# Block-causal attention and a gated MLP on one core: score visits of two head pairs joined, and two more bank pairs for the value product

## The chip, the cores and the metric

The kernel runs on one core of one Trainium2 chip. The metric is the device time of one execution in microseconds; a run is told as the median of several executions. TensorE is called PE below, ScalarE ACT, VectorE DVE, GpSimd POOL, and SyncE, which issues most of the loads, SP.

## The reference

Block-causal attention (blocks of 64 positions) over 8 batches of 8 heads, 576 positions, head size 64, is followed by an MLP over all 4608 rows:

```python
scores = scale * np.matmul(q, k.transpose(0, 1, 3, 2))
mask = block_i >= block_j
scores = np.where(mask, scores, -1000000000.0)
attn = np.exp(scores - max) ; attn = attn / (sum(attn) + 1e-09)
attn_out = np.matmul(attn, v)
x = attn_out.transpose(0, 2, 1, 3).reshape(B * S, H * D)      # 4608 x 512
h = x @ w_in                                                   # 512 -> 2048
g = h * (1.0 / (1.0 + np.exp(-beta * h)))
out = g @ w_out                                                # 2048 -> 512
```

## The kernel before

**A planner writes the order.** The Python code first makes a list of operations (`P.op`), each with the engine that may run it, an estimated duration, what it depends on, the tiles that it uses and a priority. `Plan.schedule` then plays the clock forward: whenever an engine is free it takes, of the operations that are ready and whose buffers are free, the one with the lowest priority number. A tile gets its buffer when the first operation that uses it is placed, and gives it back after its last user. The result is one fixed order for each engine, with semaphore waits between engines. So a small edit to priorities, buffers or estimates can change the order of everything after it. An operation with another array shape (mode "row" for scoring, "full" for the rest) is held back by 0.25 of priority and planned with 140 ns on top (`SWITCH`).

**Attention.** The 8 heads of a batch are 4 pairs; u counts the 32 pairs, and pairs u and u+1 with even u are called a couple here. A couple shares the tile QKT, into which Q and K come transposed: in batches 0 and 1 by PE, from batch 2 (`QB`) on by a transposing DMA on SP (line 664), after casts on POOL (line 657). Per pair PE scores in four groups (lines 673 to 703, the matmuls in `fq` on line 696, and on line 440 where a loaded weight is used again): group 0 is the first block of 128 keys with its first 512 queries, group 1 its last 64 queries and the second key block, group 2 the third and fourth blocks, group 3 the last 64 keys. The two heads of a pair use the upper and the lower 64 rows of the array at the same time. Groups 0 to 2 use array tiles of 64 rows by 128 columns, group 3 tiles of 64 by 64. From batch 1 on the groups are placed as two operations, called visits here: (0, 1) and (2, 3). ACT then takes the exponential of each group (lines 710 and 722) into a tile E, of which there are three, DVE zeroes the masked corners (716, 718), PE multiplies by V (748, 30 matmuls), DVE takes the reciprocal of the row sums and normalises (760, 767), and the result xq is turned into xT: by PE (787) up to batch 2, by a transposing DMA on SP (774) from batch 3 on.

**MLP.** The 4608 rows are 9 chunks of 512. A chunk has 16 hidden groups of four matmuls (line 971), each followed by tanh on ACT (981) and a multiply on DVE (985). Chunk 0 then uses plain matmuls with w_out (1007); chunks 1 to 8 use a scheme with seven products of half-size blocks, each in two halves of eight matmuls (892), which needs sums of blocks on DVE (856) and additions when results are taken out of the banks (913 on ACT, 916 on DVE). Chunk r's hidden groups need xT of all batches that its rows come from; for chunks 3 to 7 that is batch r.

**PSUM.** There are eight banks. Scoring groups 0 to 2 and the value product take a tile "PP" of two neighbouring banks. A scoring PP may be on banks 0-1 or 2-3 (the lower pairs); the value product too from batch 1 on (except pair 3). Everything else (group 3, hidden groups, products) takes single banks "P1" of the upper four, 4 to 7; near the end, when no PP is left to place, of all eight. Of the products two sums stay in their banks over several products (tiles Z and Y, line 929).

**Priorities.** `pr(u)` (line 435) is 994 + 100 (b - 1.5) + 4.9 c for pair c of batch b from batch 2 on. The visit (0, 1) has pr(u) + .1, (2, 3) has pr(u) + .2, the value product pr(u) + .4. Hidden group j of chunk r has 1000 + 100 r + j, and most products of chunk r come at 1103 + 100 r and later. Batch b's attention thus stands ahead of the hidden groups of chunk b - 1 and behind those of chunk b - 2, and MLP work fills PE wherever attention waits.

The lines that place the visits and the value product:

```python
            te = P.tile("EX" if u == 3 else "E")
            ...
            for grp in GROUPS[b]:
                pst = [P.tile("PP" if g0 < 3 else "P1") for g0 in grp]
                ...
                o = P.op("PE", n, fq, deps=cps, tiles=pst + [tqk] + [te] * (b > 0),
                         lat=n + 200, mode="row", prio=pr(u) + .1 + .1*(grp[0] >= 2))
            ...
            pv.at = (4, 6, 0, 2) if u == 3 else (4, 6) if b < 1 else (0, 2)
```

Of the kernel before, what the change touches and what calls it, by code (L numbers as in the profile page):

```python
# [4 lines left out]
ACT = mybir.ActivationFunctionType  # L5
# [354 lines left out]
def bass_blockwise_causal_attn__then__act_swish_beta_kernel(  # L360
# [10 lines left out]
    with es:  # L371
# [4 lines left out]
        QB, XB, CAST = 2, 3, "POOL"  # L376
        NE = 3
        PARTS = [((0, 4, "SP", range(6)), (4, 8, "SP", range(2)), (4, 8, "POOL", range(2, 6)))] + [((0, 8, "SP", range(6)),)] * 7
        GROUPS = [((0,), (1,), (2,), (3,))] + [((0, 1), (2, 3))] * 7
        NS = 6  # L380
        NO = 4
        FAST = range(1, NRC)
        RX = 5 * RC
# [11 lines left out]
        QKT = [sb(f"QKT{i}", [128, 2, 2, 640], bf16) for i in range(3)]  # L395
# [5 lines left out]
        E4 = [e[:, 3072:3136] for e in Ef]  # L401
# [12 lines left out]
        PS = es.enter_context(nc.psum_tensor("PS", [128, 8, 512], f32))  # L414
# [4 lines left out]
        P = Plan()  # L419
# [15 lines left out]
        def pr(u):  # L435
            b, c = divmod(u, NPAIR)
            return u if b < 1 else 10 * u if b < 2 else 994 + 100 * (b - LAG) + 4.9 * c
        def again(g, o, i, x):

            return g.add_instruction(mybir.InstMatmult(  # L440
                start_tensor_calc=True, stop_tensor_calc=True, tile_size=i.tile_size, tile_position=i.tile_position,
                ldweights=False, name=nc.get_next_instruction_name(), engine=i.engine,
                ins=[g.lower_ap(x), i.ins[1]], outs=[g.lower_ap(o)]))

        def es_(te):
            return NE if te.cls == "EX" else te.slot


        def mk(fn):
            return lambda g, e: fn(g)  # L450
# [13 lines left out]
        for i in range(NQ):  # L464
# [5 lines left out]
            o = P.op("POOL", 200, mk(lambda g, i=i: g.memset(Vn[i][:, 4, :, 64:66], 0.0)), prio=-5)  # L470
# [6 lines left out]
        for i in range(NQ, NE + 1):  # L477
# [8 lines left out]
                  deps=[bt, c2], tiles=[tb], lat=400, mode="full", prio=5)  # L486
# [24 lines left out]
        for i in range(NFILL):  # L511
# [10 lines left out]
            n = 125  # L522
            o = P.op("PE", n, ff, deps=[c2, c4], tiles=[tf], lat=n, mode="full", prio=1e6 + i)
# [6 lines left out]
        for b in range(B):  # L530
            ts, t = P.tile("Vs"), P.tile("V")
# [3 lines left out]
            for h0, h1, e, tt in PARTS[b]:  # L535

                vs = []
                for i in tt:
# [9 lines left out]
                    n = (h1 - h0) / 8 * (1 if i < 4 else 0.25)  # L548
                    if e == "SP":
                        o = P.op("SP", 300 + 550 * n, fv, tiles=[ts], xfer=1400 * n,  # L550
                                 prio=3.5 + 0.1 * (h0 > 0) if b == 0 else 4 * b + (3.5 if b < 2 else 0.5),
                                 dma=["d_V", h0, 1])
                    else:
                        o = P.op("POOL", 150 + 1450 * n, fv, tiles=[t], xfer=1400 * n, prio=-30 if b == 0 else 4 * b + (3.5 if b < 2 else 0.5), dma=["d_VP", h0, 1])
# [8 lines left out]
                n = 5 if 4 in tt else len(tt)  # L563
                for g0 in range(h0, h1, 2):
                    g1 = g0 + 2

                    def fw(g, e, ts=ts, t=t, g0=g0, g1=g1, n=n):
                        return g.tensor_copy(Vn[t.slot][:, 0:n, g0:g1, 0:64], Vs[ts.slot][:, 0:n, g0:g1, :])  # L568

                    o = P.op("POOL", 60 + 60 * n * (g1 - g0), fw, deps=[*vs, *ones, *vzero], tiles=[ts, t],  # L570
                             prio=4 * b + 0.5 - (38.5 - 5 * (h0 > 0)) * (b < 1))
# [23 lines left out]
        for u in range(NU):  # L595
            b, c = divmod(u, NPAIR)
            Tv = tl[b]
            p = c % 2
# [5 lines left out]
            if b < QB:  # L604

                turned = []
                for w, (nm, src) in enumerate((("Q", q), ("K", k))):
# [7 lines left out]
                    o = ld[nm, u] = P.op("SP", 420, fl, tiles=[ts], xfer=1170, prio=u, dma=["d_S", 0, 1])  # L615
                    o.pkt = 80.0

                    def fn(g, e, ts=ts, tn=tn, p=p, w=w):
# [4 lines left out]
                    o = P.op("POOL" if onp else "DVE", 850 if onp else 750, fn, deps=[o], tiles=[ts, tn],  # L623
                             prio=-40 + 3 * u if onp else -1)

                    def ft(g, e, tn=tn, pt=pt, p=p, w=w):
                        for i in range(6):
# [4 lines left out]
                    o = P.op("PE", 6 * 43, ft, deps=[o, c4], tiles=[tn, pt, tt_], lat=6 * 43 + 170, mode="full",  # L632
                             prio=pr(u))
# [6 lines left out]
            elif p == 0:  # L640

                for w, (nm, src) in enumerate((("Q", q), ("K", k))):
                    ts = P.tile("S4")

                    def fl(g, e, ts=ts, src=src, b=b, c=c):
# [3 lines left out]
                    o = P.op("SP", QKI, fl, deps=[o for t in early6 for o in t.users] if b == QB else [],  # L649
                             tiles=[ts], xfer=QKX, prio=u, dma=["d_S4", 0, 1])  # L650
# [15 lines left out]

                turned = [P.op("SP", 3250, ft, deps=casts, tiles=[tt_, tn], xfer=3200, prio=-1, dma=["d_T", 0, 1])]
            tqk, cps = tt_, turned
            te = P.tile("EX" if u == 3 else "E")
            ex = []  # L670
            zs = []
            qk = {}
            for grp in GROUPS[b]:
                pst = [P.tile("PP" if g0 < 3 else "P1") for g0 in grp]

                def fq(g, e, pst=pst, grp=grp, tqk=tqk, p=p, b=b):
                    keep = {}
                    for g0, ps in zip(grp, pst):

                        held = g0 == 1 and 0 in grp  # L680
                        blocks = {0: [(0, 0, 512, 0)], 1: [(0, 512, 576, 448), (1, 128, 576, 0)],
                                  2: [(2, 256, 576, 0), (3, 384, 576, 320)], 3: [(4, 512, 576, 0)]}[g0]
                        for t, q0, q1, off in blocks:
                            m = min(128, 576 - 128 * t)
                            for h in range(2):
                                r = slice(64 * h, 64 * h + 64)
                                if g0 < 3:
                                    o = PS[0:m, ps.slot + h, off:off + q1 - q0]
                                else:
                                    o = PS[r, ps.slot, 0:64]  # L690
                                y = 64 * h * (b >= QB)
                                x = QKT[tqk.slot][r, p, 0, q0 + y:q1 + y]
                                if held and t == 0:
                                    z = again(g, o, keep[h], x)
                                    continue
                                z = g.matmul(o, QKT[tqk.slot][r, p, 1, 128 * t + y:128 * t + m + y], x)  # L696
                                if t == 0:
                                    keep[h] = z.ins
                    return z

                n = sum(220 if g0 < 3 else 60 for g0 in grp)
                o = P.op("PE", n, fq, deps=cps, tiles=pst + [tqk] + [te] * (b > 0),
                         lat=n + 200, mode="row", prio=pr(u) + .1 + .1*(grp[0] >= 2))
                for g0, ps in zip(grp, pst):
                    qk[g0] = o, ps
            for g0 in range(4):
                o, ps = qk[g0]
                if g0 < 3:
                    def fe(g, e, ps=ps, g0=g0, te=te):
                        return g.activation(E3[es_(te)][:, g0, :, :], PS[:, ps.slot:ps.slot + 2, :], ACT.Exp,  # L710
                                            scale=0.125)
                    x = P.op("ACT", act_t(1024), fe, deps=[o], tiles=[ps, te], lat=act_t(1024) + 93, prio=0)

                    def fz(g, e, g0=g0, te=te):
                        if g0 < 2:
                            return g.memset(E3[es_(te)][64:128, g0, :, 0:64], 0.0)  # L716
                        a = E3[es_(te)][64:128, 2, :, 0:64]
                        return g.memset(bass.AP(a.tensor, a.offset, [a.ap[0], [512, 2], [320, 2], [1, 64]]), 0.0)  # L718
                    zs.append(P.op("DVE", 160 if g0 < 2 else 220, fz, deps=[x], tiles=[te], prio=-20))
                else:  # L720
                    def fe(g, e, ps=ps, te=te):
                        return g.activation(E4[es_(te)][:], PS[:, ps.slot, 0:64], ACT.Exp, scale=0.125)
                    x = P.op("ACT", act_t(64), fe, deps=[o], tiles=[ps, te], lat=act_t(64) + 93, prio=0)
                ex.append(x)

# [11 lines left out]
            if u == 3:  # L737
                spare = te
            pv = P.tile("PP")
            pv.at = (4, 6, 0, 2) if u == 3 else (4, 6) if b < 1 else (0, 2)  # L740
            ti, tx = P.tile("inv"), P.tile("xq")

            def fav(g, e, te=te, pv=pv, Tv=Tv, c=c):
                for h in range(2):
                    for i in range(5):
# [7 lines left out]
                      lat=30 * 34 + 180, mode="full", prio=pr(u)+.4 + 5 * (b < 1))  # L753
# [8 lines left out]
            r = P.op("DVE", 150, fr, deps=[av], tiles=[pv, ti], prio=0)  # L762
# [6 lines left out]
            m = P.op("DVE", dve_t(640), fm, deps=[av, r], tiles=[pv, ti, tx], prio=0)  # L769
            m.same = [r]  # L770
            nrm = [m]
            if b >= XB:
                def fy(g, e, tx=tx, c=c, b=b):
# [4 lines left out]
                n = len(blocks(b))  # L778
                xt.append(P.op("SP", 1300 * n, fy, deps=nrm + (xt[u - 4:u - 3] if b > XB else []), tiles=[tx], xfer=1100,
                               prio=-1, dma=[f"d_TX{n}_", 0, n]))  # L780
# [179 lines left out]
        for r in range(NRC):  # L960
            row = RC * r
# [4 lines left out]
            for j in range(NJ):  # L966
                ph, tt = P.tile("P1"), P.tile("th")

                def fh(g, e, ph=ph, j=j, row=row):
                    for c in range(4):  # L970
# [4 lines left out]
                o = P.op("PE", 4 * mm(512), fh, deps=xd + [win[j // 4]], tiles=[ph, tg], lat=4 * mm(512) + 170,  # L975
                         mode="full", prio=1000 + 100 * r + j)
# [21 lines left out]
            for w, d0, d1 in [(w, 0, DM) for w in range(4)]:  # L998
# [4 lines left out]
                o = None  # L1003
                for j0, j1 in parts:
                    def fo(g, e, po=po, tg=tg, w=w, j0=j0, j1=j1, d0=d0, d1=d1):
                        for j in range(j0, j1):
# [4 lines left out]
                    n = (j1 - j0) * mm(d1 - d0)  # L1011
                    was = o
                    o = P.op("PE", n, fo, deps=gs[j0:j1] + wout[j0 // 4:(j1 + 3) // 4],
                             tiles=[po, tg], lat=n + 170, mode="full",
                             prio=1000 + 100 * r + (16 + w + 0.01 * j0 if w == 0 else
                                                     103 + 5.33 * (w - 1) + 1.33 * j0 / 4))
# [84 lines left out]
```

## Time and profile before

| what | us |
|---|---|
| median of 6 runs | 337.13 (336.88 to 341.67) |
| the profiled execution, its own time | 336.88 |
| its span in the trace | 335.0 |
| PE busy | 326.4 (97%) |
| DVE busy | 220.7 (66%) |
| ACT busy | 211.2 (63%) |
| POOL busy | 84.0 (25%) |
| exponentials of groups 0 to 2 (line 710), 93 of them | 91.8, 1.025 each |
| tanh (line 981), 144 | 96.5, 0.693 each |
| multiply after tanh (line 985), 144 | 95.5, 0.681 each |
| last scoring visit begins | 256.6 |

The profile is one execution, recorded by the hardware. The span is the time from its first to its last instruction; what lies between the span and the execution's own time is start and end of the program. A group of the profile is one line's instructions of one kind: how many, the union of their times, the mean of one in ns, and the idle time of the engine ahead of them with what ended it. Matmuls overlap in their pipeline, so their recorded durations add up to more than the time they take; the distance from one start to the next is the better measure, and the timeline merges neighbours of one line into one row with the first start, the length and the count. "PEld" is the loading of weights on PE, which runs beside its matmuls.

### The profile page before, as it was taken

The page shows a single profiled execution, that of the slowest core. Times are in us where ns is not written, and L with a number is a line of the kernel's source. Part 1 is how long each engine was busy: PE and PEld are TensorE (multiplying, and loading weights), DVE is VectorE, ACT ScalarE, POOL GpSimd, SP SyncE. Part 2 cuts the span into 40 slices and gives each one's busy share as a digit, 9 for nine tenths or more (in the row PEclk, how much of TensorE's full clock was granted, in tenths as well). Part 3 has the DMA queues.
Part 4 walks back from the last instruction along what each step waited for, and adds up shares of the span by engine and source line. Part 5 has one row for each costly group of instructions (what it writes and reads, how often), then busy time and mean ns, then how long its engine had stood idle before and what let it go on. Part 6 is the DMA issues. An engine that isn't in the chain of part 4 may idle for free.

```text
span 335.0 us, 7500 instructions
## 1 busy us (share of the span) xinstructions
PE 326.4 (97%) x3148; PEld 204.1 (61%) x3092; DVE 220.7 (66%) x449; ACT 211.2 (63%) x314; POOL 84.0 (25%) x127
## 2 busy tenths in 40 slices
PE   7999999999999999999999998999999999999996
PEld 4565465445576556756566674567556766666685
DVE  4647875668655788349875865577476866666742
ACT  2855974397665885686788557765877545544521
POOL 7656081055064027205320540510000000000000
PEclk9999999999999999999999999999999999999999
DMA  7999999899999999989699999975121201110023
GB/s 198 222 242 233 191 219 206 171 257 224 197 256 214 207 235 208 217 169 244 124 222 205 184 269 197 198 142 99 33 54 39 84 31 33 40 55 31 5 92 125
DMA packets 154993, 53.41 MB, mean 159 GB/s; under 512 B 139072, under 2 KB 154448, under 8 KB 154960
## 3 DMA queue, kind: packets, MB, share of 16 engines
q1 hardware_dynamic: 141200, 40.19, 63.9%
q10 hardware_dynamic: 8192, 8.39, 8.3%
q0 software_dynamic: 5568, 4.36, 8.3%
q8 instruction: 24, 0.39, 0.5%
q14 instruction: 9, 0.07, 0.1%
HBM read 36.71 MB, written 9.44 MB: 138 GB/s over the span
## 4 chain that ended last, share of the span: by engine, by line
PE 90%; DVE 3%; DMA 3%; ACT 2%; SPq 1%; issue 0%; POOL 0%
PE PS L971 37%; PE PS L892 29%; PE PS L748 9%; PE PS L696 8%; PE PS L1007 4%; DMA ST<-in_k_dram 2%; PE PS L519 2%; PE PS L787 1%; DVE gT L985 1%; ACT E L710 1%; PE PS L628 1%; DVE xq L767 1%; DMA xT<-xq 1%; SPq L612 1%; ACT th L981 1%
## 5 line engine op out<-in xcount | busy, mean ns | idle before, releaser
L971 PE MATMUL PS<-xT,w_in 128*128 128x512 bf16 x576 | 137.4, 380 | 1.3 <-DVE E L718 1.0
L981 ACT ACTIVATE th<-PS,beta 128x512 f32<-128x512 f32 x144 | 96.5, 693 | 64.6 <-PE PS L971 61.2
L985 DVE SCALAR_TENSOR_TENSOR gT<-th,PS 128x512 f16<-128x512 f32 x144 | 95.5, 681 | 40.0 <-ACT th L981 39.5
L710 ACT ACTIVATE E<-PS 128x1024 bf16<-128x1024 f32 x93 | 91.8, 1025 | 23.2 <-PE PS L696 22.4
L971 PEld LDWEIGHTS PS<-xT,w_in 128*128 128x128 bf16 x576 | 52.6, 98 | 57.7 <-issue 3.4
L892 PE MATMUL PS<-w_out,gT 128*128 128x256 f16 x512 | 63.2, 273 | 0.0
L892 PEld LDWEIGHTS PS<-w_out,gT 128*128 128x128 f16 x512 | 48.8, 98 | 11.8 <-DVE gT L985 0.6
L657 POOL CAST QKn<-ST 128x640 bf16<-128x640 f32 x48 | 36.8, 768 | 31.5 <-DMA ST<-in_k_dram 22.8
L568 POOL CAST Vn<-Vs 128x640 bf16<-128x640 f32 (+1 forms) x28 | 20.9, 746 | 91.5 <-DMA Vs<-in_v_dram 90.3
L696 PE MATMUL PS<-QKT 64*128 64x512 bf16 (+4 forms) x328 | 37.1, 297 | 0.4 <-DVE xq L767 0.3
L748 PEld LDWEIGHTS PS<-Vn,E 128*128 128x128 bf16 x930 | 31.5, 97 | 4.2 <-DVE xq L767 0.6
L913 ACT ACTIVATE ost<-PS 128x512 f32<-128x512 f32 x32 | 19.2, 599 | 22.8 <-PE PS L892 22.7
L748 PE MATMUL PS<-Vn,E 128*128 128x65 bf16 x930 | 32.8, 193 | 0.5 <-DVE xq L767 0.5
L892 PE MATMUL PS<-OV 128*128 128x256 f16 x256 | 32.1, 273 | 0.0
L696 PEld LDWEIGHTS PS<-QKT 64*128 64x128 bf16 (+1 forms) x328 | 13.4, 95 | 27.2 <-issue 15.8
L892 PEld LDWEIGHTS PS<-OV 128*128 128x128 f16 x256 | 24.3, 98 | 6.1 <-issue 0.4
L767 DVE TENSOR_TENSOR xq<-PS,inv 128x640 bf16<-128x640 f32 x32 | 26.2, 819 | 0.6
L716 DVE MEMSET E<- 64x64 uint32 x62 | 6.9, 112 | 26.2 <-ACT E L710 24.4
L856 DVE TENSOR_TENSOR OV<-gT 128x1024 f16<-128x1024 f16 x32 | 22.5, 710 | 1.1 <-PE PS L892 0.6
L916 DVE SCALAR_TENSOR_TENSOR ost<-PS,ost 128x512 f32<-128x512 f32 x22 | 15.1, 685 | 5.5 <-PE PS L892 4.8
L892 PE MATMUL PS<-OV,gT 128*128 128x256 f16 x128 | 16.0, 273 | 0.0
L1007 PE MATMUL PS<-w_out,gT 128*128 128x512 f16 x64 | 15.3, 380 | 0.0
(61 smaller groups left out, 174.7 us busy)
## 6 DMA issues: line engine op xcount, KB each, us to landing
out_dram<-ost ACTq DMA_DIRECT2D x32, 256.0 KB, 3.2
ST<-in_q_dram SPq DMA_DIRECT2D x12, 576.0 KB, 6.0
ST<-in_k_dram SPq DMA_DIRECT2D x12, 576.0 KB, 7.8
Vs<-in_v_dram SPq DMA_DIRECT2D x24, 256.0 KB, 4.6
ST<-in_q_dram SPq DMA_DIRECT2D x8, 288.0 KB, 6.2
ST<-in_k_dram SPq DMA_DIRECT2D x8, 288.0 KB, 6.8
w_in<-in_moe_w_in_dram POOLq DMA_DIRECT2D x4, 512.0 KB, 10.9
w_out<-in_moe_w_out_dram POOLq DMA_DIRECT2D x4, 512.0 KB, 10.0
```

What stands on the lines that cost most here:

```text
L568: return g.tensor_copy(Vn[t.slot][:, 0:n, g0:g1, 0:64], Vs[ts.slot][:, 0:n, g0:g1, :])
L657: return g.tensor_copy(QKn[tn.slot][:].rearrange("p a w n -> p (a w n)")[:, 640 * (2 * a + w):][:, 0:640] .rearrange("p (t h d) -> p t h d ...
L696: z = g.matmul(o, QKT[tqk.slot][r, p, 1, 128 * t + y:128 * t + m + y], x)
L710: return g.activation(E3[es_(te)][:, g0, :, :], PS[:, ps.slot:ps.slot + 2, :], ACT.Exp, scale=0.125)
L748: z = g.matmul(o, eblk(te, t, i, h), Vn[Tv.slot][:, t, 2 * c + h, 0:65], start=(t == 0), stop=(t == i))
L767: return g.tensor_tensor(xq[tx.slot][:].rearrange("p i (h d) -> p h i d", h=2), both(pv, 0, 64), x, ALU.mult)
L856: return P.op("DVE", dve_t(SZ * HC / 2), mk(lambda g: g.tensor_tensor(fo(), fx(), fy(), op)), deps=deps, tiles=tiles, prio=prio)
L892: x = g.matmul(PS[:, pw.slot, HM * w:HM * w + HM], fa()[:, j, 128 * w:128 * w + 128], fb()[:, j, :], start=first and (pair or w == 0) and ...
L971: z = g.matmul(PS[:, ph.slot, :], w_in[:, c, 128 * j:128 * j + 128], xT[:, c, row % RX:row % RX + RC], start=(c == 0), stop=(c == 3))
L981: return g.activation(th[tt.slot][:], PS[:, ph.slot, :], ACT.Tanh, scale=beta[:, j:j + 1])
L985: return g.scalar_tensor_tensor(out=gT[tg.slot][:, j, :], in0=th[tt.slot][:], scalar=1.0, in1=PS[:, ph.slot, :], op0=ALU.add, op1=ALU.mult)
L1007: z = g.matmul(PS[:, po.slot, 0:d1 - d0], gT[tg.slot][:, j, 128 * w:128 * w + 128], w_out[:, j, d0:d1], start=(j == 0), stop=(j == NJ - 1))
```

## The change

For batches 2 to 7 (`JOIN`) a couple's visits are placed together, when the loop is at its first pair. There are three: (0, 1) of pair u; groups 2 and 3 of u and then groups 2 and 3 of u+1 in one operation; (0, 1) of pair u+1. The middle one has priority pr(u) + .2, the others pr(u) + .1 and pr(u+1) + .1. It takes two PP tiles and a single bank that both pairs' group 3 share (64 columns each), and the E tiles of both pairs. The exponential of group 3 reads its pair's 64 columns. The value product of batches 2 to 7 may be placed on banks 4-5 or 6-7 if neither lower pair is free. All matmuls, exponentials and transfers are the same in number and shape. In batches 0 and 1 the visits are as before; only group 3 of an odd pair uses the other 64 columns of its bank.

```diff
+        JOIN = (2,3,4,5,6,7)
...
-            te = P.tile("EX" if u == 3 else "E")
...
-            for grp in GROUPS[b]:
-                pst = [P.tile("PP" if g0 < 3 else "P1") for g0 in grp]
...
-                n = sum(220 if g0 < 3 else 60 for g0 in grp)
-                o = P.op("PE", n, fq, deps=cps, tiles=pst + [tqk] + [te] * (b > 0),
-                         lat=n + 200, mode="row", prio=pr(u) + .1 + .1*(grp[0] >= 2))
+            if b not in JOIN or p == 0:
+                tes = {uu: P.tile("EX" if uu == 3 else "E") for uu in ((u,) if b not in JOIN else (u, u + 1))}
+                qks = {uu: {} for uu in tes}
+                visits = [[(u, g) for g in grp] for grp in GROUPS[b]] if b not in JOIN else [
+                    [(u, 0), (u, 1)], [(u, 2), (u, 3), (u + 1, 2), (u + 1, 3)], [(u + 1, 0), (u + 1, 1)]]
+                for grp in visits:
+                    small = P.tile("P1") if any(g0 == 3 for _, g0 in grp) else None
+                    pst = [P.tile("PP") if g0 < 3 else small for _, g0 in grp]
...
+                                    if g0 < 3:
+                                        o = PS[0:m, ps.slot + h, off:off + q1 - q0]
+                                    else:
+                                        o = PS[r, ps.slot, 64 * (uu % 2):64 * (uu % 2) + 64]
...
+                    n = sum(220 if g0 < 3 else 60 for _, g0 in grp)
+                    o = P.op("PE", n, fq, deps=cps, tiles=list({id(x): x for x in pst}.values()) + [tqk] + [tes[uu] for uu in sorted({uu for uu, _ in grp})] * (b > 0),
+                             lat=n + 200, mode="row", prio=pr(u) + .2 if len(grp) == 4 else pr(u + 1) + .1 if grp[0][0] > u else
+                             pr(u) + .1 + .1 * (grp[0][1] >= 2))
...
-                        return g.activation(E4[es_(te)][:], PS[:, ps.slot, 0:64], ACT.Exp, scale=0.125)
+                        return g.activation(E4[es_(te)][:], PS[:, ps.slot, 64 * p:64 * p + 64], ACT.Exp, scale=0.125)
...
-            pv.at = (4, 6, 0, 2) if u == 3 else (4, 6) if b < 1 else (0, 2)
+            pv.at = (4, 6, 0, 2) if u == 3 else (4, 6) if b < 1 else (0, 2, 4, 6) if b in JOIN else (0, 2)
```

More of the change, by code (lines that the diff above doesn't have):

```diff
@@ L668, in bass_blockwise_causal_attn__then__act_swish_beta_kernel @@
             tqk, cps = tt_, turned
-            te = P.tile("EX" if u == 3 else "E")
             ex = []
             zs = []
-            qk = {}
-            for grp in GROUPS[b]:
-                pst = [P.tile("PP" if g0 < 3 else "P1") for g0 in grp]
[L676 to L699, printed above, removed]
-                n = sum(220 if g0 < 3 else 60 for g0 in grp)
-                o = P.op("PE", n, fq, deps=cps, tiles=pst + [tqk] + [te] * (b > 0),
-                         lat=n + 200, mode="row", prio=pr(u) + .1 + .1*(grp[0] >= 2))
-                for g0, ps in zip(grp, pst):
-                    qk[g0] = o, ps
@@ new lines, in bass_blockwise_causal_attn__then__act_swish_beta_kernel, with fq @@
+            if b not in JOIN or p == 0:
[6 more added lines that the diff above has]
+                    pst = [P.tile("PP") if g0 < 3 else small for _, g0 in grp]
+                    def fq(g, e, pst=pst, grp=grp, tqk=tqk, b=b):
+                        keep = {}
+                        for (uu, g0), ps in zip(grp, pst):
+                            held = g0 == 1 and (uu, 0) in grp
+                            blocks = {0: [(0, 0, 512, 0)], 1: [(0, 512, 576, 448), (1, 128, 576, 0)],
+                                      2: [(2, 256, 576, 0), (3, 384, 576, 320)], 3: [(4, 512, 576, 0)]}[g0]
+                            for t, q0, q1, off in blocks:
+                                m = min(128, 576 - 128 * t)
+                                for h in range(2):
+                                    r = slice(64 * h, 64 * h + 64)
+                                    if g0 < 3:
+                                        o = PS[0:m, ps.slot + h, off:off + q1 - q0]
+                                    else:
+                                        o = PS[r, ps.slot, 64 * (uu % 2):64 * (uu % 2) + 64]
+                                    y = 64 * h * (b >= QB)
+                                    x = QKT[tqk.slot][r, uu % 2, 0, q0 + y:q1 + y]
+                                    if held and t == 0:
+                                        z = again(g, o, keep[h], x)
+                                        continue
+                                    z = g.matmul(o, QKT[tqk.slot][r, uu % 2, 1, 128 * t + y:128 * t + m + y], x)
+                                    if t == 0:
+                                        keep[h] = z.ins
+                        return z
+                    n = sum(220 if g0 < 3 else 60 for _, g0 in grp)
+                    o = P.op("PE", n, fq, deps=cps, tiles=list({id(x): x for x in pst}.values()) + [tqk] + [tes[uu] for uu in sorted({uu for uu, _ in grp})] * (b > 0),
+                             lat=n + 200, mode="row", prio=pr(u) + .2 if len(grp) == 4 else pr(u + 1) + .1 if grp[0][0] > u else
+                             pr(u) + .1 + .1 * (grp[0][1] >= 2))
+                    for (uu, g0), ps in zip(grp, pst):
+                        qks[uu][g0] = o, ps
@@ L706, in bass_blockwise_causal_attn__then__act_swish_beta_kernel @@
+            te, qk = tes[u], qks[u]
             for g0 in range(4):
@@ L720, in bass_blockwise_causal_attn__then__act_swish_beta_kernel, with fe @@
                 else:
-                    def fe(g, e, ps=ps, te=te):
-                        return g.activation(E4[es_(te)][:], PS[:, ps.slot, 0:64], ACT.Exp, scale=0.125)
+                    def fe(g, e, ps=ps, te=te, p=p):
+                        return g.activation(E4[es_(te)][:], PS[:, ps.slot, 64 * p:64 * p + 64], ACT.Exp, scale=0.125)
                     x = P.op("ACT", act_t(64), fe, deps=[o], tiles=[ps, te], lat=act_t(64) + 93, prio=0)
```

## The prediction

> **What bounds the kernel now.** I read the page first: busy shares, clock row, chain.
>
> ```profile
> span 335.0 us, 7500 instructions
> ...
> PE 326.4 (97%) x3148; PEld 204.1 (61%) x3092; DVE 220.7 (66%) x449; ACT 211.2 (63%) x314; POOL 84.0 (25%) x127
> ...
> PEclk9999999999999999999999999999999999999999
> ...
> PE 90%; DVE 3%; DMA 3%; ACT 2%; SPq 1%; issue 0%; POOL 0%
> ...
> L710 ACT ACTIVATE E<-PS 128x1024 bf16<-128x1024 f32 x93 | 91.8, 1025 | 23.2 <-PE PS L696 22.4
> ...
> L767 DVE TENSOR_TENSOR xq<-PS,inv 128x640 bf16<-128x640 f32 x32 | 26.2, 819 | 0.6
> ```
>
> PE is busy 97% at an undisturbed clock and holds 90% of the chain of waits. Batches 0 and 1 are untouched, so the stretch that matters begins with the first visit of batch 2, at 67 us. Stage table, from there to the end of attention and on to the end (columns: PE, PEld, DVE, ACT, POOL busy, clock, DMA):
>
> ```profile
> 67.00:262.00 195.00, 193.27 (x1939) 118.37 (x1889) 132.58 (x277) 139.92 (x208) 52.55 (x68) 1.00 0.95 180
> 262.00:335.00 73.00, 70.25 (x507) 49.18 (x505) 45.07 (x71) 32.16 (x49) 0.00 (x0) 1.00 0.18 57
> ```
>
> PE lacks 1.7 us of 195; ACT and DVE are at 72% and 68%. After 262 us PE runs projections alone. So the time is PE's work plus PE's waits, and only two things can move it: how long PE takes for a visit, and where it stands still. That attention finishes earlier or later is worth nothing in itself, because hidden groups and products fill PE meanwhile.
>
> "Busy" hides the losses inside a visit, so I went to the starts of single matmuls in the trace. Full-array matmuls start 0.109 us apart at 256 columns and 0.216 at 512. What exceeds that is a wait or a change of tile shape. From 67 us on ten waits of over 0.06 us add up to 2.9: 1.20 at 204.55, 0.37 at 102.50, 0.37 at 166.10, the other seven 1.0 together.
>
> **The switch, measured.** Two single visits of groups 2 and 3, with eight products' matmuls between them (timeline of PE):
>
> ```profile
> 127.81 1.80 PE L892 MATMUL PS<-w_out,gT 128*128 128x256 f16 x15
> 129.54 0.54 PE L696 MATMUL PS<-QKT 64*128 64x320 bf16 x6
> 130.02 1.05 PE L892 MATMUL PS<-w_out,gT 128*128 128x256 f16 x8
> 131.00 0.54 PE L696 MATMUL PS<-QKT 64*128 64x320 bf16 x6
> 131.47 0.72 PE L892 MATMUL PS<-w_out,gT 128*128 128x256 f16 x5
> ```
>
> From 130.02 to 131.00 is 0.98; eight matmuls are 0.87; so entering the visit costs 0.10. From 129.54 to 130.02 is 0.47 (unrounded). A single visit therefore costs 0.57. The plan of before already puts two such visits back to back three times (near 90, 175 and 201.5 us). One of them:
>
> ```profile
> 174.46 0.59 PE L971 MATMUL PS<-xT,w_in 128*128 128x512 bf16 x2
> 174.99 1.01 PE L696 MATMUL PS<-QKT 64*128 64x320 bf16 x12
> 175.93 0.50 PE L892 MATMUL PS<-w_out,gT 128*128 128x256 f16 x3
> ```
>
> From 174.99 to 175.93 is 0.94, plus 0.10 for the entry: 1.04. This is exactly the twelve-matmul middle visit of the change, so its price needs no guess: 2 x 0.57 - 1.04 = 0.10 saved.
>
> **The change, part by part.**
>
> *Visits joined.* No matmul is added or removed. Twelve couples of pairs (batches 2 to 7, two each) go from four visits to three. Counting a visit as one entry (0.10) and one exit (0.12 after a 64x64 tile), twelve would save 12 x 0.22 = 2.6 us. The Trainium skill speaks against that count: its page "TensorEngine Tiling (Array Packing)", section "Tiling Modes", says that changing the tile shape makes the array drain. In a visit the shape changes again, since groups 0 to 2 use 64x128 tiles and group 3 uses 64x64. The trace agrees: 64x128 to 64x64 costs 0.09, and in the row at 174.99 the step from pair u's 64x64 tiles to pair u+1's 64x128 costs 0.12, as much as a leave would. Listed as (2, 3, 2, 3), the joined visit has five shape changes where two single ones have six. I take the row: 0.097 each. Three of the twelve are joined already, so nine are gained: 9 x 0.097 = **0.87 us**, all on PE, which sets the end. By the entry-and-exit count on all twelve the time would be 334.5.
>
> *Order.* In before, groups 2 and 3 of both pairs often run between the two pairs' groups 0 and 1 already, so the change mostly fixes an order that is there. Moved earlier with the joined visit is pair u+1's E slot: two of three slots are taken at once. No DMA is reordered by the code: loads on SP keep their priority, V's casts stay on POOL, and the transposes of Q and K serve both pairs of a couple already. Hidden by PE's fill; if the cover goes, a late E slot delays the next couple's first visit by at most a value product with normalising, about 2 us of attention, not of PE.
>
> *A new wait.* Groups 2 and 3 needed one lower pair of banks; joined they need both, and one upper bank. So the visit may wait for one exp more, 1.02 (L710), and its own first exp starts 0.47 later (0.94 of PE, not 0.47). That is 0.5 to 1.5 us per couple, 1 to 3 us per batch. Behind it in the schedule stand exps, the value product (L748), normalising, the transposing DMA (L774), then the hidden groups (L971) of the chunk that needs the batch. PE itself is given other work by the planner, which knows these banks; counting L892's matmuls in the trace, 5 to 12 products of 0.87 of the earlier chunks are still undone when chunks 3 to 6 begin. On PE I take **0**; bounds below.
>
> *Value products on upper banks.* They can start without waiting for a scoring pair. The wait that this could remove is the one at 102.50, whose releaser is the normalising that empties a lower pair:
>
> ```profile
> 102.50 0.39 PE L696 MATMUL PS<-QKT 64*128 64x512 bf16 x2 [0.30 <-DVE xq L767]
> ...
> 166.10 0.82 PE L971 MATMUL PS<-xT,w_in 128*128 128x512 bf16 x3 [0.20 <-DMA xT<-xq]
> ...
> 199.90 2.17 SPq L774 DMA_TRANSPOSE xT<-xq  x1
> ...
> 204.55 0.81 PE L971 MATMUL PS<-xT,w_in 128*128 128x512 bf16 x3 [1.03 <-DVE E L718]
> ```
>
> It is worth 0.37, with 0.07 at 96.92. In exchange an upper pair is gone for 0.92 (L748) + 0.22 (L760) + 0.82 (L767) + about 0.1 between them = 2.1 us. The lower pairs come first in the list, so I expect few upper ones. I take 0; bounds -0.4 and +4.8 (the squeeze, below).
>
> The named releaser at 204.55 misleads: hidden groups don't read E. The last transpose of batch 5 was issued at 199.90 and landed 4.6 us later, at 204.5. So that wait, like 166.10, is for xT.
>
> **Sum.** Span 335.0 - 0.87 = 334.1; 1.9 lies around it (336.88 - 335.0): 336.0 for the profiled execution. The median of the runs is 0.25 above that execution, so **336.3 us**. The waits of 2.9 us bound the unknown downwards; with all of them gone it would be 333.4.
>
> **Rivals.**
>
> *Waits go too.* An upper bank is freed (one for both group 3s, not two), scoring doesn't wait for normalising, and xT comes in time at 166 and 204.5. For it: those waits total 2.0 us and depend on the order. Against: a new order makes waits of its own, and the planner's order of before already leaves only 1.1% of this stretch. Time: 337.1 - 0.87 - 2.0 = 334.2.
>
> *xT late.* The joined visit's longer chain makes chunks 3 to 6 start on an xT that the planner believed landed. For it: the plan counts 0.56 for this visit's matmuls, and 0.95 for an exp that takes 1.025; 204.55 shows that a misjudged landing costs 1.2. Against: the misjudged part is only about 0.5 per visit, and the planner puts undone products in front while it waits for xT. If all four boundaries cost 1.2: 4.8 in place of 1.6, so +3.2 - 0.87: 339.4, still within 1%.
>
> *Bank squeeze (the other side).* Place: the upper four banks. The products' sums (line 929) hold one or two for many visits, a value product takes two for 2.1 us, and then no hidden group can start. The same page of the skill, section "Restrictions and Gotchas", says that row tiling raises the pressure on PSUM since each row tile writes a bank of its own; five of eight banks now go to one visit. It gives no price; the rows do: of 2.1, PE spends 0.92 on the value product and 0.87 on a product, if one is ready, leaving 0.3 to 0.4 idle, and 1.2 if none is. With 12 of the 24 up there at 0.4 each, 4.8 - 0.87 = +3.9: 341.1. It makes the change a loss once these idles pass 0.87, and a loss of over 1% once they pass 4.2. Against: an upper pair is taken only when both its banks are free.
>
> *No change at all.* If the plan, unasked, had joined as many, nothing would be gained; it did so three times of twelve, so at least nine are new.
>
> **Chances.** Forecast 0.5 (335.2 to 337.6, waits between -1.1 and +1.3 of today's), waits go 0.15, xT late 0.2, squeeze 0.15. A measurement of this kernel can tell about 1% from no change, that is 3.4 us: below 333.8 lies only the end of the second case, 0.04; above 340.5 the squeeze and the tail of xT late, 0.14; within, 0.82. The range takes in most of the second and third cases: 334.0 to 340.4.
>
> **What would show it.** Right: no scoring visit of group 2 alone after 67 us, twelve visits of twelve matmuls of 1.04 each, nine visits fewer, PE's waits after 67 us still near 3 us. Wrong: waits before L971 released by L985 or L767 (banks: squeeze); waits before the first L971 of a chunk when an L774 lands (xT late); joined visits that cost other than 1.04; PE's streaming time changed. If the time moves by over 1 us, I expect waits to account for it, not switches.

## The result, and the profile after

The changed kernel takes 335.99 us in the median (35 runs) beside 337.54 us for the kernel before in the same comparison: a ratio of 0.9951, 95% interval 0.9935 to 0.9967. That is about 1.65 us, where 0.87 was forecast. (The ratio leaves out the few executions that took over 1.5% longer than their kernel's quickest; the medians, over all, differ by 1.55.) Line numbers have moved: loads of Q and K are L647 (was L646), scoring is L701 (was L696), and from there on lines stand seven later: exponentials L717, the value product L755, normalising L774, the transposing DMA of xT L781, products L899, hidden groups L978, their multiply L992 (L993 in the kernels with a hold).

The page of the changed kernel:

```profile
span 332.9 us, 7496 instructions
...
PE 324.3 (97%) x3148; PEld 204.4 (61%) x3092; DVE 220.0 (66%) x449; ACT 210.4 (63%) x314; POOL 84.6 (25%) x127
...
PE 83%; DMA 5%; ACT 4%; DVE 3%; SPq 2%; issue 1%; POOL 0%; ACTq 0%
```

PE's busy time fell by 2.1 us, just as the span did, and it is still busy 97%: the bound is the same. The share of DMA in the chain that ended last rose from 3% to 5%.

One joined visit on PE's timeline:

```profile
183.79 1.04 PE L899 MATMUL PS<-w_out,gT 128*128 128x256 f16 x8
184.76 1.01 PE L701 MATMUL PS<-QKT 64*128 64x320 bf16 x12
185.70 1.04 PE L978 MATMUL PS<-xT,w_in 128*128 128x512 bf16 x4
```

Eight matmuls at 0.109 begin at 183.79, so the visit costs 0.10 to enter and 0.94 until the next full matmul starts. Twelve visits of twelve matmuls stand in the trace (three before) and no visit of groups 2 and 3 of one pair is left after 67 us.

I split the stretch from the first visit of batch 2 to the start of PE's last matmul into waits (distance between two starts, less streaming, less the shape change; those over 0.06 us) and the rest. Distances that fit one matmul missing from the trace are left out of the waits.

| us | to last matmul | waits | rest |
|---|---|---|---|
| before | 264.4 | 2.9 | 261.5 |
| changed | 262.5 | 2.2 | 260.3 |

The stretch is 1.9 shorter: 1.15 in the rest, 0.75 in waits. The other 0.3 of the span's 2.1 lies ahead of batch 2, where the two kernels do the same work, and says nothing of the change. In the rest, nine visits saved are 9 x 0.097 = 0.87; a further 0.2 comes from one joined visit that follows directly on a PE transpose of 64 rows (103.69 us), so that neither a leave nor an entry is paid there. The waits changed places more than they shrank. For 166.10 (0.37) and 204.55 (1.20) there are now 0.24 at 168.81 and 0.53 at 205.49, both for xT, and a new one of 0.59 at 77.07, where a hidden group waits for the multiply L992, which gives a bank back (the last xT that chunks 4 and 5 need landed at 168.76 and 205.44, just ahead of the two):

```profile
77.07 0.61 PE L978 MATMUL PS<-xT,w_in 128*128 128x512 bf16 x2 [0.43 <-DVE gT L992]
...
168.81 0.61 PE L978 MATMUL PS<-xT,w_in 128*128 128x512 bf16 x2
...
205.49 0.82 PE L978 MATMUL PS<-xT,w_in 128*128 128x512 bf16 x3 [0.37 <-DMA xT<-xq]
```

The bracket shows only the idle part after the modelled end of the matmul before; the distances between starts give the larger numbers above.

### The profile page after: what moved, and what is told of

The parts are those of the page before. It is cut to its first block, busy times and chain, and to the rows that moved or that the text cites. A ratio compares the mean times of both kernels' runs of the same rounds, so it can differ in the third digit from the quotient of the medians.

```text
span 332.9 us, 7496 instructions
## 1 busy us (share of the span) xinstructions
PE 324.3 (97%) x3148; PEld 204.4 (61%) x3092; DVE 220.0 (66%) x449; ACT 210.4 (63%) x314; POOL 84.6 (25%) x127
## 4 chain that ended last, share of the span: by engine, by line
PE 83%; DMA 5%; ACT 4%; DVE 3%; SPq 2%; issue 1%; POOL 0%; ACTq 0%
PE PS L978 35%; PE PS L899 26%; PE PS L755 8%; PE PS L701 7%; PE PS L1014 4%; ACT E L717 3%; DMA Vs<-in_v_dram 2%; DMA xT<-xq 2%; SPq L543 1%; PE PS L794 1%; ACT th L988 1%; DMA ST<-in_k_dram 1%; DVE gT L992 1%; PE PS L629 1%; DVE OV L863 1%
## 5 line engine op out<-in xcount | busy, mean ns | idle before, releaser
L978 PE MATMUL PS<-xT,w_in 128*128 128x512 bf16 x576 | 137.3, 380 | 1.0 <-DVE gT L992 0.4
L992 DVE SCALAR_TENSOR_TENSOR gT<-th,PS 128x512 f16<-128x512 f32 x144 | 95.9, 681 | 36.8 <-ACT th L988 35.9
L717 ACT ACTIVATE E<-PS 128x1024 bf16<-128x1024 f32 x93 | 91.8, 1026 | 28.6 <-PE PS L701 28.0
L978 PEld LDWEIGHTS PS<-xT,w_in 128*128 128x128 bf16 x576 | 52.7, 98 | 56.9 <-DVE gT L992 2.4
L899 PE MATMUL PS<-w_out,gT 128*128 128x256 f16 x512 | 63.3, 273 | 0.0
L899 PEld LDWEIGHTS PS<-w_out,gT 128*128 128x128 f16 x512 | 49.1, 98 | 12.5 <-issue 0.8
L658 POOL CAST QKn<-ST 128x640 bf16<-128x640 f32 x48 | 38.0, 792 | 23.6 <-DMA ST<-in_k_dram 12.9
L701 PE MATMUL PS<-QKT 64*128 64x320 bf16 (+4 forms) x328 | 36.5, 297 | 0.4 <-ACT E L717 0.4
L755 PEld LDWEIGHTS PS<-Vn,E 128*128 128x128 bf16 x930 | 31.1, 97 | 3.7 <-DVE xq L774 0.6
L755 PE MATMUL PS<-Vn,E 128*128 128x65 bf16 x930 | 32.2, 193 | 0.7 <-DVE xq L774 0.5
L899 PE MATMUL PS<-OV 128*128 128x256 f16 x256 | 32.1, 273 | 0.0
L701 PEld LDWEIGHTS PS<-QKT 64*128 64x128 bf16 (+1 forms) x328 | 13.4, 95 | 25.6 <-issue 10.3
L899 PEld LDWEIGHTS PS<-OV 128*128 128x128 f16 x256 | 24.6, 98 | 6.3 <-issue 0.6
L774 DVE TENSOR_TENSOR xq<-PS,inv 128x640 bf16<-128x640 f32 x32 | 26.2, 819 | 0.6
L725 DVE MEMSET E<- 64x128 uint32 x31 | 5.1, 165 | 18.0 <-ACT E L717 17.0
L899 PE MATMUL PS<-OV,gT 128*128 128x256 f16 x128 | 16.0, 273 | 0.0
```

The source lines that it names most:

```text
L658: return g.tensor_copy(QKn[tn.slot][:].rearrange("p a w n -> p (a w n)")[:, 640 * (2 * a + w):][:, 0:640] .rearrange("p (t h d) -> p t h d ...
L701: z = g.matmul(o, QKT[tqk.slot][r, uu % 2, 1, 128 * t + y:128 * t + m + y], x)
L755: z = g.matmul(o, eblk(te, t, i, h), Vn[Tv.slot][:, t, 2 * c + h, 0:65], start=(t == 0), stop=(t == i))
L774: return g.tensor_tensor(xq[tx.slot][:].rearrange("p i (h d) -> p h i d", h=2), both(pv, 0, 64), x, ALU.mult)
L899: x = g.matmul(PS[:, pw.slot, HM * w:HM * w + HM], fa()[:, j, 128 * w:128 * w + 128], fb()[:, j, :], start=first and (pair or w == 0) and ...
L978: z = g.matmul(PS[:, ph.slot, :], w_in[:, c, 128 * j:128 * j + 128], xT[:, c, row % RX:row % RX + RC], start=(c == 0), stop=(c == 3))
```

## The experiments

**Each half alone.** Theory S holds that the gain is saved shape changes. Theory B holds that it needs the upper banks.

```diff
-            pv.at = ... else (0, 2, 4, 6) if b in JOIN else (0, 2)
+            pv.at = (4, 6, 0, 2) if u == 3 else (4, 6) if b < 1 else (0, 2)
```

> The joined visits alone; the value product stays on the two lower pairs of banks. Theory S (the gain is nine visits' worth of tile-shape changes, 0.87 us, and waits that happen to be 0.7 us shorter): still below before, about 336.5, ratio 0.997. Theory B (the gain needs the upper bank pairs, because a joined visit wants both lower pairs at once and would otherwise wait for a value product to be normalised): the saved switches are eaten by new waits on PE ahead of L701's first matmul, 338 or more, ratio 1.001 or more.

Measured: ratio 1.0056 (1.0030 to 1.0082), median 339.93. Joined visits without the upper banks make the kernel slower. PE's timeline near chunk 3, in this kernel's quickest execution (336.67), shows what the saving went into:

```profile
141.83 0.39 PE L701 MATMUL PS<-QKT 64*128 64x512 bf16 x2
...
144.47 0.39 PE L701 MATMUL PS<-QKT 64*128 64x512 bf16 x2 [2.04 <-ACT E L717]
...
146.20 1.07 PE L755 MATMUL PS<-Vn,E 128*128 128x65 bf16 x30 [1.12 <-ACT E L717]
147.12 0.38 PE L978 MATMUL PS<-xT,w_in 128*128 128x512 bf16 x1
```

PE goes from one scoring visit to the next with 2.0 us of nothing between, then idles 1.1 us more: it has no MLP work at all. The last xT of batch 3, issued at 141.17, landed at 146.62, and at 147.12, after the value product, chunk 3's first hidden group starts. Counting L899's matmuls before it (a product here is a half of eight matmuls), no product of the earlier chunks was left; in the kernel before, five were left at that boundary. So this is the rival "xT late" at one boundary, with the reserve used up, though in another form: the wait stands ahead of scoring and the value product, not ahead of a hidden group. Away from its waits (4.4 us) the stretch is 260.1, as in the changed kernel: the shape changes were saved here too.

In this execution the waits just eat up the saving: 264.5 us to the last matmul, beside 264.4 before. The loss that the median shows goes with the clock. Only 3 of the 22 executions have a mean granted clock of 0.998 or more (median 337.61); nine lie at 0.995 (339.35), ten at 0.990 or below (about 340.6). Of the 67 executions of before beside them, 46 are at 0.998 or more (337.07); of the changed kernel, 31 of 36 (335.69), so the change as a whole gains 1.4 there. One spell at half clock as long as that of the last section, 3.4 us, would lower the mean over 335 us by 0.005, by an estimate from that trace, so one or two such spells would do. Which waits bring them on here isn't shown, as no trace of such an execution was kept.

The other half:

```diff
-            pv.at = (4, 6, 0, 2) if u == 3 else (4, 6) if b < 1 else (0, 2)
+            pv.at = (4, 6, 0, 2) if u == 3 else (4, 6) if b < 1 else (0, 2, 4, 6) if b >= 2 else (0, 2)
```

> The upper bank pairs alone: four visits for two pairs of heads as before, the value product of batches 2 to 7 may take banks 4-5 or 6-7 when no lower pair is free. Theory S: no visit is saved, so 337.5 like before (ratio 0.999 to 1.001). Theory B: the waits of scoring for normalising go, 0.4 to 0.8 us, ratio about 0.998.

Measured: ratio 0.9997 (0.9968 to 1.0026), and in the trace 3.1 us of waits and a rest of 261.4, both nearly as before. Alone the upper banks are worth nothing that can be measured. They are hardly used either: in the fixed order of this kernel one value product of the 24 of batches 2 to 7 stands there. The halves don't add up: +1.9 and 0 make -1.65 together. Theory S is right on what is saved, theory B on what makes it count.

**Which placement it is.** In its fixed order the changed kernel puts only two of the 24 value products on upper banks: the last pair's of batch 2, near 101 us, and one in batch 4, planned near 148 us. I closed the upper banks for all but batch 2:

```diff
-            pv.at = ... else (0, 2, 4, 6) if b in JOIN else (0, 2)
+            pv.at = ... else (0, 2, 4, 6) if b == 2 else (0, 2)
```

> The changed kernel with the upper bank pairs open to the value products of batch 2 alone; one of them, the last pair's, then uses one. Theory P (that one placement near 101.5 us is what separates the changed kernel from the joined visits alone: without it batch 3's first joined visit stands behind a value product and its normalising, xT of batch 3 lands 8 us later, and chunk 3 starts with no product left to fill PE): 336.0 like the changed kernel, ratio 0.995. If the upper banks help in several batches: between 336 and 339.5, about 338, ratio 1.001.

Measured: ratio 0.9922 (0.9894 to 0.9950). One placement is enough. Up to it the changed kernel, this one and the joined visits alone have the same order of operations. Here it is in the changed kernel, and then the same place in the kernel with joined visits alone:

```profile
100.17 0.39 PE L701 MATMUL PS<-QKT 64*128 64x512 bf16 x2 [0.19 <-ACT E L717]
...
100.70 1.08 PE L755 MATMUL PS<-Vn,E 128*128 128x65 bf16 x30
101.62 1.47 PE L899 MATMUL PS<-w_out,gT 128*128 128x256 f16 x12
```

```profile
99.78 0.39 PE L701 MATMUL PS<-QKT 64*128 64x512 bf16 x2 [0.18 <-ACT E L717]
...
100.32 1.92 PE L899 MATMUL PS<-w_out,gT 128*128 128x256 f16 x16
102.08 1.07 PE L755 MATMUL PS<-Vn,E 128*128 128x65 bf16 x30
```

Batch 3's first visit has just taken both lower pairs. On upper banks the value product follows it at once; on lower banks it first waits out the exponentials, and then batch 3's joined visit waits out its normalising, because it wants both pairs. Batch 3 stays behind from there: its joined visit begins at 103.69 in the changed kernel and at 105.06 without the placement, and its last xT lands at 138.55 and at 146.62.

**The squeeze at full dose.** All 24 value products of batches 2 to 7 on upper banks:

```diff
-            pv.at = ... else (0, 2, 4, 6) if b in JOIN else (0, 2)
+            pv.at = ... else (4, 6) if b in JOIN else (0, 2)
```

> The changed kernel with all value products of batches 2 to 7 forced onto banks 4-5 or 6-7 (two dozen of them). The rival of the prediction, the bank squeeze, at full dose: 24 times 0.4 us of PE idle ahead of hidden groups, about +9.6 us on the changed kernel: 345. If products fill PE all the same and the squeeze has no price: 336, since scoring then has the lower pairs for itself.

Measured: ratio 1.0067 (1.0042 to 1.0092), 1.2% above the changed kernel's ratio: some 3.9 us, not 9.6. All that the edit does thus costs about 0.18 us for each of the 22 further placements, where I had put 0.4 for the squeeze alone. The three largest waits of PE from 66 us on in its profiled execution, which took 345.80 beside a median of 340.46 (columns: who waited for what, total us, times, longest):

```profile
PE PS L978 <- DMA xT<-xq: 3.4, 1, 3.4
PE PS L899 <- ACT ost L920: 2.1, 3, 0.7
PE PS L978 <- DVE gT L992: 1.5, 2, 1.0
```

The third line is the squeeze as I had described it, hidden groups without a bank: 1.5 us. The second is new: PE comes to a product before ACT has read out an earlier sum. The first is xT late in landing. This execution lost more than the median did, so how the 3.9 us divide among the three isn't shown.

**The joined visit sorted by tile shape.** If the price of a visit is its shape changes, the order 2, 3, 2, 3 wastes two of five:

```diff
-                    [(u, 0), (u, 1)], [(u, 2), (u, 3), (u + 1, 2), (u + 1, 3)], [(u + 1, 0), (u + 1, 1)]]
+                    [(u, 0), (u, 1)], [(u, 2), (u + 1, 2), (u, 3), (u + 1, 3)], [(u + 1, 0), (u + 1, 1)]]
```

> The changed kernel with the joined visit's groups listed as 2, 2, 3, 3 in place of 2, 3, 2, 3. The order of operations on every engine and all banks are those of the changed kernel; only within the joined visit three tile-shape changes are left of five. Theory S: each of the twelve visits takes 1.04 - 0.12 - 0.09 = 0.83 us, together 2.5 us less on PE: 333.5, ratio to before 0.988. If a change of shape inside a visit is hidden by the weight loads, or if waits take up what is saved: 336, like the changed kernel, ratio 0.995.

Measured: ratio 0.9915 (0.9888 to 0.9942), median 334.74. The visit does what was expected, from 189.84 to 190.56 with the entry 0.82 us for 1.04:

```profile
188.87 1.04 PE L899 MATMUL PS<-w_out,gT 128*128 128x256 f16 x8
189.84 0.79 PE L701 MATMUL PS<-QKT 64*128 64x320 bf16 x12
190.56 1.04 PE L978 MATMUL PS<-xT,w_in 128*128 128x512 bf16 x4
```

Yet of 12 x 0.22 = 2.65 us only some 1.2 reach the time (1.6 between the executions at a mean clock of 0.998 or more: 334.13 beside 335.69). The profiled execution, which took 338.15, shows a place where gains can go: chunk 4 waits for xT, and for longer than in any trace above.

```profile
172.28 3.52 PE L978 MATMUL PS<-xT,w_in 128*128 128x512 bf16 x8 [4.03 <-DMA xT<-xq]
```

Theory X: PE comes earlier to the hidden groups of chunks 4 and 5, but xT doesn't. Its transposes stand in SP's queue behind loads. SP's rows in the changed kernel and then in this execution:

```profile
156.83 4.07 SPq L647 DMA_DIRECT2D ST<-in_k_dram  x1
160.94 6.71 SPq L781 DMA_TRANSPOSE xT<-xq  x4
```

```profile
161.26 2.65 SPq L647 DMA_DIRECT2D ST<-in_k_dram  x1
163.96 7.17 SPq L781 DMA_TRANSPOSE xT<-xq  x4
```

A load keeps SP for 2.7 to 4.1 us here, and the four transposes begin when it is out, 3 us later in the second (1.2 of the 3 were there already at the first visit of batch 2). I gave PE products to do in the meantime: the hidden groups of chunks 4 and 5 are held back after the moment at which the planner believes that xT has landed.

```diff
+                o.rest = 2000.0 if r in (4, 5) else 0.0
                 hs.append(o)
```

On the sorted visits:

> The changed kernel with the joined visit sorted by tile shape (2, 2, 3, 3), and the hidden groups of chunks 4 and 5 held back by 2 us after the moment at which the planner believes xT landed, so that products fill PE there. Theory X (the sorted visit alone gained 1.2 of 2.65 us because PE, being earlier, only waits longer for xT, whose transposing DMA it doesn't hasten): with the hold the whole 2.65 us and the changed kernel's waits of 0.77 for xT come out, 332.6, ratio to before 0.986. If the missing part went elsewhere: 334.7 as without the hold, ratio 0.9915.

Measured: ratio 0.9892 (0.9847 to 0.9936), median 334.44: nearer the second expectation, 334.7, though the interval takes in both. Its waits on PE still have xT on top, so the hold was too short:

```profile
PE PS L978 <- DMA xT<-xq: 2.7, 2, 2.0
```

On the changed kernel's visits:

> The changed kernel, joined visit unsorted, with the same hold of chunks 4 and 5. Theory X: its waits of 0.24 and 0.53 us ahead of the hidden groups of chunks 4 and 5 go, 335.2, ratio to before 0.993. If a held hidden group only moves the wait: 336.0, ratio 0.995.

Measured: ratio 0.9910 (0.9878 to 0.9942), median 334.53. No wait for xT is left in the trace and the waits fall to 1.0 us, as expected; the time fell somewhat more than the expected 0.8, within the intervals.

A hold of 4000 in place of 2000, with sorted visits and with those of the changed kernel; apart from the order inside the visit the two have the same order of operations:

> Joined visits sorted by tile shape, hidden groups of chunks 4 and 5 held for 4 us in place of 2 us. With 2 us PE still waited 2.2 and 0.8 us for xT in the trace, since PE runs ahead of the planner's clock. Theory X: with 2.5 and 0.8 us more of products in front these waits go, and the sorted visits keep their 2.65 us: 331.5, ratio to before 0.983. If the gain of sorting is lost elsewhere: 334.5, ratio 0.991.

> The same order of operations, banks and hold, with the joined visit in the order of the changed kernel (2, 3, 2, 3). It stands beside the sorted one and differs by nothing but two changes of tile shape in each of twelve visits. Theory X: 12 x 0.22 = 2.65 us longer than the sorted one, 334.2, ratio to before 0.991. If sorting is worth nothing once PE waits: both the same.

Measured: 333.77, ratio 0.9876 (0.9836 to 0.9917), and 334.60, ratio 0.9913 (0.9883 to 0.9942). The difference of the medians is 0.8 and the intervals overlap, so by time alone the 2.65 isn't shown. The traces tell why. Waits of PE with sorted visits, then with the others:

```profile
PE PS L978 <- DMA xT<-xq: 1.1, 1, 1.1
PE PS L978 <- DVE gT L993: 0.9, 2, 0.8
```

```profile
PE PS L978 <- DVE gT L993: 0.7, 2, 0.5
```

At chunk 5 the sorted kernel again comes to an xT that hasn't landed (1.24 us from start to start at 206.56), while the other finds it there. The traces with joined visits and an undisturbed clock side by side, as in the table above:

| us | visits | to last matmul | waits | rest |
|---|---|---|---|---|
| joined, lower banks only | 2,3,2,3 | 264.5 | 4.4 | 260.1 |
| changed, upper in batch 2 only | 2,3,2,3 | 261.9 | 1.5 | 260.3 |
| changed, hold 2 us | 2,3,2,3 | 261.3 | 1.0 | 260.2 |
| changed, hold 4 us | 2,3,2,3 | 262.2 | 1.9 | 260.3 |
| sorted, hold 2 us | 2,2,3,3 | 261.5 | 4.4 | 257.1 |
| sorted, hold 4 us | 2,2,3,3 | 260.8 | 3.4 | 257.4 |

The rest is 260.1 to 260.3 wherever visits are joined as 2,3,2,3, and 2.7 to 3.2 less where they are sorted (2.65 of it is read directly from the visits). Waits then take 1.5 to 3.4 of it back, and in both sorted kernels it is mostly the wait for xT that grew. So the gain is there on PE and goes into waiting, but theory X tells only a part of why. Counted from the first visit of batch 2, the last xT of batch 4 landed at 103.3 to 103.7 us in the three sorted traces and at 100.3 to 101.8 in the four unsorted ones with upper banks; that of batch 5 at 137.8 to 140.7 and at 134.0 to 138.1. With the long hold PE was ready for chunk 5 at 137.0 in the sorted kernel; had xT landed at 136.3, as it did in the other, nothing would have waited. So xT not only came no earlier, it came later. Whether sorting brings this on, or the chance of single executions, is not shown, and why a load keeps SP for so long, and so what would bring xT earlier, stays open. Sorted visits with the long hold are the best version here and beat both kernels: 0.9876 of before, about 4 us.

## Why the prediction was right, and where not

**The price of a shape change held.** 0.097 per visit and nine visits, 0.87 us, were taken from a visit of this kind that the trace of before had by chance. The changed kernel's visits measure 1.04 as predicted, and the rest of PE's time fell by 1.15. The entry-and-exit count would have given 2.6, or 2.0 on the nine visits. Sorting is the proof from the other side: with three changes for five the same twelve matmuls take 0.82, 0.22 less, as the 0.12 and 0.09 of the prediction add up to.

**"Order", that the change mostly fixes an order that is there, was only half right.** In the changed kernel both pairs' groups 0 and 1 come before the joined visit in several couples (the first couple: visits at 67.3 and 70.6 us, the joined one at 74.7). I saw no price of its own for this.

**"A new wait", taken as 0 on PE, held for the change as a whole, but not for the reason given.** The reason was 5 to 12 products in reserve at the boundaries of chunks 3 to 6. At chunk 3 the changed order uses up its five. What keeps PE busy is that xT of batch 3 comes early enough, and this hangs on the other half of the change. With joined visits alone PE stands still for 3.4 us at that boundary, and the gain is gone.

**"Value products on upper banks", taken as 0, is the step that was mis-sized.** Beside visits that aren't joined it is 0. Beside joined ones it is worth the difference between 1.0056 and 0.9951, about 3.5 us, and one placement of 24 does it; 2.0 of this stand in the traces at undisturbed clock (264.5 beside 262.5 us), the rest goes with the lowered clock of most executions without it. I priced the two edits one by one; their price is that of the pair. The bound of -0.4 for it looked at a wait in before, and the wait that it removes exists only after the other edit. The new wait and the placement that removes it were both taken as 0; that they cancel in the sum was luck.

**The waits.** They fell by 0.75, inside the band of the forecast (-1.1 to +1.3), and moved. The band gave no sign, so that 0.75 of the stretch's 1.9 came from waits was not foreseen. Of the rival "waits go too" it is a part. The rival "xT late" didn't happen in the changed kernel: its two waits for xT add up to 0.77 where before had 1.56. It did in the joined visits alone and in the sorted ones. Of the bank squeeze the changed kernel shows at most the 0.59 at 77.07, which stands ahead of any value product on upper banks in these batches; with all 24 there the loss was 3.9 us in all, under half of the price that I gave to the squeeze alone.

## What to carry to other kernels

Price a visit to another tile shape by the number of shape changes inside and around it, from the starts of single matmuls, and when visits are joined, sort the work in them by shape. When an edit makes an operation want more buffers at once, look for the edit that gives buffers back and price the two together, at the place where the reserve of other work is smallest. Where an engine is full and its next input comes over a queue that it doesn't drive, time saved on the engine can turn into waiting until that input comes earlier or other work is put in front.

## What the runs showed of the hardware

A long wait can cost PE twice. In the execution with sorted visits in which PE waited 4.0 us for xT, the next eight matmuls of 512 columns started 0.43 us apart, not 0.216. The stage table (PE, PEld, DVE, ACT, POOL busy, granted clock, DMA) has the clock at half for 3.4 us:

```profile
168.00:172.20 4.20, 0.25 (x9) 0.12 (x5) 2.26 (x5) 0.00 (x0) 2.09 (x3) 1.00 0.33 67
172.20:175.60 3.40, 3.32 (x8) 1.20 (x9) 0.68 (x1) 0.69 (x1) 0.00 (x0) 0.50 1.48 176
175.60:180.00 4.40, 4.40 (x40) 2.71 (x37) 1.13 (x5) 3.44 (x5) 0.00 (x0) 1.00 1.05 212
```

That is 1.7 us lost on top of the wait. With all value products on upper banks, a wait of 3.4 us was followed by a longer spell:

```profile
179.00:182.50 3.50, 0.20 (x2) 0.00 (x0) 0.00 (x0) 0.60 (x1) 0.00 (x0) 0.89 0.71 188
182.50:188.60 6.10, 5.99 (x17) 2.45 (x18) 1.38 (x2) 2.03 (x3) 2.49 (x4) 0.51 1.11 227
```

That is some 3 us lost. The waits of 2.0 us in the joined visits alone and in the sorted ones with the short hold left no such mark (clock 1.00). The Trainium skill's "TensorE: Matmul & The Clock Gate" ("Why this matters for your kernels") names gaps of over about 3 us as the point where the clock falls; these traces lie on either side of it.
